# A two-layer mixture kernel on one core: its written order of issue chosen anew, with 54 engine choices changed

## The chip, the cores and the metric

The kernel runs on one core of one Trainium2 chip. The core has TensorE (PE, which multiplies matrices; its weight loads are listed as PEld), VectorE (DVE), ScalarE (ACT), GpSimd (POOL) and SyncE (SP), which here issues all loads and stores between the chip's memory (HBM) and the core's own memories: SBUF, and PSUM into which PE writes its products. The metric is the time of one execution in microseconds (us). Before the change it was 584.19 us, the median of three runs (582.6 to 584.66).

## What is computed

From `x` [4, 8, 512, 64] and `state` [4, 8, 32, 64] attention is computed in both directions; the results are joined into 4 x (512 + 32) = 2176 tokens of 512 values, and two layers follow:

```python
xread = softmax(x @ state.T / 8) @ state
sread = softmax(state @ x.T / 8) @ x
t = concat(xread, sread)               # 2176 tokens x 512
h = t @ w_in                           # 512 -> 1024
solu = h * softmax(h)
ln = (solu - mean(solu)) / sqrt(var(solu) + 1e-6) * g_ln
y = ln @ w_out                         # 1024 -> 512
h2 = y @ w2_in                         # 512 -> 2048
out = (h2 * tanh(softplus(h2))) @ w2_out   # 2048 -> 512
```

All of it is single precision. The weights arrive as 64-bit floats and are turned into 32-bit floats on the chip.

## The kernel before, in words

**Precision.** PE multiplies `fp32r` numbers, so each operand is kept as a high part and a rest (`..h` and `..l` in the names), and each product is three matmuls: low by high, high by high, high by low.

**Narrowing.** `narrow` (lines 144 to 166) makes 32-bit floats of a block of 128 x 512 words of 64 bits. The high word is rescaled (line 149 on DVE or line 151 on ACT: flag W), the low word is shifted (154 ACT, 156 DVE: flag B), and the two are joined, either by a cast on ACT (159) and one instruction on DVE (161), or by two on DVE (161, 165: flag T). The blocks of the first layer are numbered 0 to 11, those of the second 12 to 27.

**First layer.** 17 tiles of 128 tokens. Attention (lines 303 to 490) turns scores and results on DVE (STREAM_TRANSPOSE, lines 381 and 411) and leaves `aT`. `s_a0` (511) multiplies it with `w_in` (line 530). `s_a1` (535) applies softmax and normalization (lines 539 to 562; small steps on DVE, ACT or POOL by flags N and Z). `s_turn` and `s_turn_far` transpose the result: on PE, split by lines 579 and 581, or through DRAM, with a store (590) and four loads (595) for each tile. `s_d` (608) multiplies blocks of up to four tiles with `w_out` (24 matmuls, line 616) and evicts PSUM into `raw_*` by line 621, on ACT or DVE (flag X). The PSUM of `s_d`, `s_warm` and others is one ring. `s_warm` (236) multiplies unused numbers early on, so that PE is not idle: its call 0 has 26 matmuls, each further one 4, or none by flag R.

**Second layer.** The 2048 middle values are taken in eight steps `fp` of 256, and the tokens in three passes of 6, 6 and 5 tiles. In pass 0 the weights of a step are loaded (`s_load64(which, f)`, line 640: 512 KB each, `which` 0 for `w2_in`, 1 for `w2_out`, two blocks f for a step), narrowed, summed for a Strassen-Winograd scheme of 7 products (657), split into high part and rest (681, 683, 717, 719, 724, 726), and kept in DRAM for the later passes (687, 730, 733). Passes 1 and 2 fetch them from there (694, 745). Each step has 42 matmuls (`s_hp`, line 860). `s_post` (869) evicts and combines the products: `m` (line 871, ACT or DVE: flag M), `u` (874, 877), `c` (882). `s_act` (885) makes value and split (894 and 901 on ACT, 905 on DVE or POOL: flag L). Pass 0 then runs `s_po` (lines 915 to 917), with an output copy `ob` (921, flag S) and store (923). Passes 1 and 2 use sums (931, DVE or POOL: flag J), splits (939, 941), blocks (965 to 967) and running sums on DVE (972). `s_x_split` (lines 792, 794) prepares the tokens of a pass.

**What sets the order.** Nothing is scheduled by the compiler. Each engine runs its instructions in the order in which they were issued, and so does SP's queue. Every step above is a generator, which issues some instructions up to its next `yield`. All steps are listed once, and a string of two-letter codes says which is advanced next:

```python
    live = {}
    with tc.manual_schedule():
        for i in range(0, len(ORDER), 2):
            n = 64 * CODE.index(ORDER[i]) + CODE.index(ORDER[i + 1])
            if n not in live:
                step, step_args = steps[n]
                live[n] = step(*step_args)
            next(live[n], None)
```

A code that comes three times advances its step three times: `Ds` is `s_load64(0, 0)`, the load first, then the narrowing piece by piece; `DY` and `Db` are `s_d(5, 0)` and `s_d(5, 3)`, of which the last advance holds the eviction. `FLAGS` holds one character for each choice of an engine, read by `eng`:

```python
def eng(name, i, *choice):
    return choice[int(FLAGS[name][i])]
```

An instruction waits for the data that it reads and for the buffer that it writes; all later ones on the same engine or queue wait behind it.

Of the kernel before, what the change touches and what calls it, by code (L numbers as in the profile page):

```python
# [22 lines left out]
P = 128
# [60 lines left out]
    "CIDQCGCoDQCGCGCoDRB3CIDRCoB3DRB3DVCIDkDkDlDVCIDlDlDRDoDVCyDRCyDqDWDoCyDWCyDqDoDoCvCzCvDqDqCvCvDpCzDpCyDpDpCzCyCv"
    "CzCzCvC2C0C2C2C0C0DWDVC0C3DWDVC0C0DXDWDXC3C0C0C5C0C3C5C5C3C1C3C3DUDXC6C1C3C3C9C3C6C4C9C9C6C4DUDUC6C-C6C6DXC-DUC6"
    "DAC1DUC6C-C6C1C1DADAC1DXC-C4C-C-C4C4DZDrDmC4C-C-DZDBDrDaC1DaC-DBDZC_DvDwDaC4DrDrC_DaDsC1DZDaDvDYDBDvDYDvDYC4DBDw"
    "DYDBDBDZC8DvDbDwDBDBD3DbDwDsD8D8DbDYDsDbDwDsDdDmDmC_C_DdD5DxC_DxC8DdC_DxDbD9D9D3D4C7DBDeEAEAC7DxDxDdD4D6DeD5DdDt"
# [4 lines left out]
    "G3EbElG5G4EbEqEqElEfEuEuG4EfG6EbG6EcEhGwGwEcEiEfEgGvGvEcEmEcEcG1G1FLG6EkEhG0G0EjG5G4EgEpEpEkEiG2G2EjEyG4FMG5FIEm"
    "G9EtEtG4G4G9G5G9G8G-G-EfEfG8G5G5E1EoHAHAExG7EsEsG8HKExEoHKEwEwG7ExFLG_G_FLE4G7HLHFHFE4EyEyHKHLEyHGHGFLEyHKEzHMEz"
    "HDHDFIFIHLHJHJFIEzEzEzHCHCFLE3HEHEE6FAE3HMFEHBHBE6FMHMHKFJE5FIFiE7FMHKFAFAHLFME5E7HRHRHLE1FfHKHKE1FEFEFME1HSHSHL"
    "HLFNHQHQHPE1HNHcHPE2E2FVFNHcHOHdFZFZFOFNHOHHHHFNFNFJHdHIHIHPFJE2HcFJFjHOFVHcHNFOFdFdHeE2E2HNHeHWHWFJFUHTHTE_HdHU"
# [1111 lines left out]
```

## Time and profile before

| | us |
|---|---|
| median of three runs (range) | 584.19 (582.6 to 584.66) |
| the profiled execution's own time | 584.61 |
| its span in the profile | 582.8 |
| PE busy | 561.5 (96%) |
| DVE busy | 500.1 (86%) |
| ACT busy | 362.3 (62%) |
| POOL busy | 53.9 (9%) |

The profile is of one execution, whose own time is 1.8 us longer than the span that it records. Busy time of PE counts overlapping matmuls once, and their ends are modelled; whether PE is fed at its rate is read from the starts of its matmuls and from its waits. By stages, the first layer and the preparation of pass 0 fill the first 240 us or so, pass 0 of the second layer reaches to about 375 us, pass 1 to about 480 us, and pass 2 to the end.

### The profile page before, as it was taken

To read this page: it belongs to the slowest core of one execution; us is meant where nothing else is said; L and a number is where in the kernel's file an instruction comes from. 1 tells how busy PE (TensorE), PEld (TensorE's weight loads), DVE (VectorE), ACT (ScalarE), POOL (GpSimd) and SP (SyncE) were. 2 spreads that over 40 slices of the span, in tenths; PEclk is the share of its full clock that TensorE was granted. 3 is DMA by queue.
4 is the path that set the end of the run, shared out by engine and by line. 5 is a ranking of instruction groups with operands and counts; after the bars stand their busy time and mean duration, and the time that the engine had idled before them with its cause. 6 is when DMAs were issued, how large, how long until landed. Compare 5 with 4: busy or idle time off the path is not lost.

```text
span 582.8 us, 9844 instructions
## 1 busy us (share of the span) xinstructions
PE 561.5 (96%) x3561; PEld 498.6 (86%) x3561; DVE 500.1 (86%) x943; ACT 362.3 (62%) x665; POOL 53.9 (9%) x132
## 2 busy tenths in 40 slices
PE   9978999999999898999999999999999999999997
PEld 3535787899789897888888899899999998999996
DVE  5999988785787888989999997388989997989995
ACT  6997868573448765989999774443334735433340
POOL 0003222120022000000000000000000034000023
PEclk9998999999999999999999999999999999999999
DMA  8952204223215677899997889777777769987932
GB/s 349 412 204 73 73 37 128 92 74 109 73 63 191 223 283 239 305 345 336 340 325 276 323 306 321 253 280 259 250 265 254 262 246 330 338 288 289 318 113 92
DMA packets 47280, 136.05 MB, mean 233 GB/s; under 512 B 5376, under 2 KB 20864, under 8 KB 46720
## 3 DMA queue, kind: packets, MB, share of 16 engines
q1 hardware_dynamic: 47232, 135.42, 65.7%
q8 instruction: 28, 0.46, 0.3%
q14 instruction: 20, 0.16, 0.1%
HBM read 96.60 MB, written 38.80 MB: 232 GB/s over the span
## 4 chain that ended last, share of the span: by engine, by line
PE 40%; ACT 11%; DVE 2%; DMA 2%; issue 1%; ACTq 0%; DVEq 0%
PE hp L860 20%; PE po L965 6%; PE po L966 5%; PE po L967 5%; ACT w L159 3%; DMA out<-ob 2%; ACT w L151 1%; PE po L1033 1%; ACT gh L901 1%; ACT w L154 1%; ACT w2oh L724 1%; ACT w2oh L717 1%; PE po L917 1%; PE po L916 1%; PE po L915 1%
## 5 line engine op out<-in xcount | busy, mean ns | idle before, releaser
L860 PE MATMUL hp<-xo,w2r 128*128 128x384 f32 (+1 forms) x504 | 94.2, 329 | 2.2 <-DVE c L882 1.7
L860 PEld LDWEIGHTS hp<-xo,w2r 128*128 128x128 f32 x504 | 84.4, 188 | 5.8 <-DVE c L882 3.2
L860 PE MATMUL hp<-xo,w2swh 128*128 128x384 f32 (+1 forms) x336 | 83.2, 330 | 3.2 <-ACT m L871 1.5
L616 PE MATMUL pm<-ln_l,gw_hi 128*128 128x256 f32 (+1 forms) x256 | 76.3, 298 | 3.9 <-ACT raw_d L621 2.4
L616 PE MATMUL pm<-ln_h,gw_hi 128*128 128x256 f32 (+1 forms) x256 | 74.8, 292 | 0.0
L616 PE MATMUL pm<-ln_h,gw_lo 128*128 128x256 f32 (+1 forms) x256 | 74.4, 291 | 0.0
L972 DVE TENSOR_TENSOR acc<-po,acc 128x384 f32<-128x384 f32 (+1 forms) x136 | 69.0, 522 | 1.8 <-PE po L967 1.2
L860 PEld LDWEIGHTS hp<-xo,w2swh 128*128 128x128 f32 x336 | 58.9, 188 | 7.4 <-ACT m L871 2.3
L901 ACT ACTIVATE gh<-c 128x384 fp32r<-128x384 f32 (+1 forms) x57 | 29.1, 515 | 57.3 <-DVE c L882 48.1
L616 PEld LDWEIGHTS pm<-ln_l,gw_hi 128*128 128x128 f32 x256 | 48.3, 189 | 8.1 <-ACT raw_d L621 3.1
L860 PE MATMUL hp<-xo,w2swl 128*128 128x384 f32 (+1 forms) x168 | 55.1, 328 | 0.0
L882 DVE TENSOR_TENSOR c<-hp,u 128x384 f32<-128x384 f32 (+1 forms) x72 | 38.2, 532 | 13.6 <-PE hp L860 13.1
L616 PEld LDWEIGHTS pm<-ln_h,gw_hi 128*128 128x128 f32 x256 | 48.2, 188 | 0.5
L616 PEld LDWEIGHTS pm<-ln_h,gw_lo 128*128 128x128 f32 x256 | 48.6, 190 | 0.0
L939 ACT CAST qh<-t 128x384 fp32r<-128x384 f32 (+1 forms) x60 | 28.5, 489 | 31.2 <-DVE t L931 20.5
L530 PE MATMUL ph<-swh,aT 128*128 128x512 f32 x128 | 41.2, 416 | 3.7 <-ACT ph L548 2.5
L965 PE MATMUL po<-ql,w2oh 128*128 128x384 f32 (+1 forms) x120 | 39.2, 327 | 0.4 <-DVE acc L972 0.4
L966 PE MATMUL po<-qh,w2oh 128*128 128x384 f32 (+1 forms) x120 | 38.8, 323 | 0.0
L967 PE MATMUL po<-qh,w2ol 128*128 128x384 f32 (+1 forms) x120 | 38.7, 323 | 0.0
L941 DVE TENSOR_TENSOR ql<-t,qh 128x384 fp32r<-128x384 f32 (+1 forms) x60 | 31.0, 533 | 1.6 <-ACT qh L939 1.2
L860 PEld LDWEIGHTS hp<-xo,w2swl 128*128 128x128 f32 x168 | 31.5, 188 | 0.1
L530 PEld LDWEIGHTS ph<-swh,aT 128*128 128x128 f32 x128 | 23.3, 194 | 9.6 <-issue 2.7
(452 smaller groups left out, 1363.4 us busy)
## 6 DMA issues: line engine op xcount, KB each, us to landing
w2r<-ki SPq DMA_DIRECT2D x16, 768.0 KB, 6.1
w2ol<-ko SPq DMA_DIRECT2D x15, 768.0 KB, 6.5
w2oh<-ko SPq DMA_DIRECT2D x15, 768.0 KB, 6.6
w<-in_w2i SPq DMA_DIRECT2D x16, 512.0 KB, 5.7
w2swh<-ki SPq DMA_DIRECT2D x8, 896.0 KB, 6.1
w2swl<-ki SPq DMA_DIRECT2D x8, 896.0 KB, 7.0
w<-in_w2o SPq DMA_DIRECT2D x12, 512.0 KB, 5.3
ki<-w2r SPq DMA_DIRECT2D x8, 768.0 KB, 7.6
```

Source lines behind the costliest of these rows:

```text
L159: nc.scalar.copy(out=src.bitcast(F16)[..., 1], in_=f32(high))
L530: nc.tensor.matmul(out=ph[:, hf * 512:(hf + 1) * 512], lhsT=a_[:, c * P:(c + 1) * P], rhs=w_[:, q, hf * 512:(hf + 1) * 512], start=q == 0 ...
L616: nc.tensor.matmul(out=pm[:, :n], lhsT=w_[:, k, m * P:(m + 1) * P], rhs=l_[:, c0:c0 + 4 * len(blk), k, :], start=k == 0 and j == 0, stop=k ...
L860: nc.tensor.matmul(out=r, lhsT=w_[:, 0, k * P:(k + 1) * P], rhs=x_[:, k, :n], start=s in (0, 1, 3, 4) and cnt == 0, stop=cnt == 5, skip_gr ...
L882: nc.vector.tensor_tensor(out=c, in0=bank[ps, fp, s], in1=u, op=ALU.add)
L901: nc.scalar.activation(out=gh, in_=src, func=AF.Mish)
L939: nc.scalar.copy(out=hi, in_=src)
L941: on('V', ((ps - 1) * NFP + fp) * 4 + int(name[1]) - 1).tensor_tensor(out=lo, in0=src, in1=f32(hi), op=ALU.subtract)
L965: nc.tensor.matmul(out=r, lhsT=wh[:, a, c], rhs=x[1], start=first or not held, stop=False)
L966: nc.tensor.matmul(out=r, lhsT=wh[:, a, c], rhs=x[0], start=False, stop=False)
L967: nc.tensor.matmul(out=r, lhsT=wl[:, a, c], rhs=x[0], start=False, stop=last or not held)
L972: on.tensor_tensor(out=o, in0=x, in1=y, op=ALU.add)
```

## The change

Only the two constants are changed; no line of code is. In `FLAGS` 54 characters differ (B 8, J 1, L 1, M 5, N 6, Q 2, R 1, S 1, T 3, W 4, X 14, Z 8), each of which gives one operation to another engine, or, for R, leaves out one `s_warm` of 4 matmuls. `ORDER` has 3158 codes instead of 3160: the two codes of `s_warm(7)` are gone, and every other step has as many codes as before, in another sequence from the first line on. In the diff one stretch of `ORDER` is shown, with the eviction of `s_d(5, 0)` and the narrowing of `s_load64(0, 0)`; the rest is cut.

```diff
 FLAGS = dict(
...
-    B="1011001100011000000001111110",
+    B="0000011100011000010010111010",
-    J="0000000000000000000000000000010000000000000000000000000000000000",
+    J="0000000000000000000000000000000000000000000000000000000000000000",
-    L="000000000000000000000000000000000000000000000000000000000000000100000000000000000000000000000000",
-    M="000110000110100001000010",
-    N="00010010100111011",
+    L="000000000000000000000000000000000000000000000000000000000000000000000000000000000000000000000000",
+    M="001100001110000000000010",
+    N="00010001110010001",
-    Q="111111111111110001010001",
-    R="0101010101110000",
-    S="000100",
-    T="1100010110001010111111111110",
+    Q="111011111111110101010001",
+    R="0101011101110000",
+    S="000110",
+    T="1101111110001010111111111110",
-    W="0001000100000001101000000000",
-    X="10000000001000011010010000000111",
+    W="1101010100000001111000000000",
+    X="00111010001100100101010001000101",
-    Z="11111110010100001",
+    Z="11101011110011101",
...
 ORDER = (
...
-    "DYDBDBDZC8DvDbDwDBDBD3DbDwDsD8D8DbDYDsDbDwDsDdDmDmC_C_DdD5DxC_DxC8DdC_DxDbD9D9D3D4C7DBDeEAEAC7DxDxDdD4D6DeD5DdDt"
...
+    "DAC1C6C1C-C1DADAC4DUC-C4C-C-C4C4DaDrC1DmC-DZDBDrC8C-DaDmDmC-DaDrDrDaDBC_DvDwDZDaC4DZDBC_C7DsC1DYC4DBDZDBDBDYDZDv"
+    "C1DYDBDBDvDYDvDbDBDwDbDYDvDbDwD3DwDbC7D8D8D3DeDsC_DwC_DbDeC_DxD5DxDdC_DsDxD9D9DxDxDdD4EAEAC7DsDdD4D5DeDtC8DsEBEB"
...
```

Told by its instructions, the stretch has this order on ACT (the step, its line):

```
before: split_out(0,0) L717, load64(0,0) L151, d(5,0) L621, load64(0,0) L154
after:  d(5,0) L621, split_out(0,0) L717, load64(0,0) L151, d(5,3) L621
```

What moves elsewhere, in the same terms:

- ahead of `s_a0(6)`: two operations of attention, `s_front_turn(2, 0)` (lines 411 and 348), are issued later, and one split, one small step and one eviction (lines 422, 546, 621) come sooner;
- between the loads and the narrowing of the second layer's weights: most of the loads are issued sooner on SP's queue, by 1.5 to 5 us of PE's work for those of the last steps. The narrowing of some is moved further still, so that it follows more closely behind its load: for `s_load64(1, 8)`, (1, 9), (1, 7), (0, 8), (0, 6), (0, 7). For (1, 0), (0, 0), (1, 3), (0, 2) it follows at a greater distance;
- `s_load64(0, 3)` stands ahead of a store of `s_keep_out(1, 1)`, and the last reader of the slot that it fills (line 726) stands sooner on DVE;
- the stores of the outputs of pass 0's last step (line 923) stand ahead of the two loads of `s_fetch_in(1, 2)` (line 694), which come later;
- passes 1 and 2 have nearly their old order.

## Rows read from the trace of the kernel before

**Rows 1.** The page, first line and part 1: busy us (share) xinstructions.

```profile
span 582.8 us, 9844 instructions
PE 561.5 (96%) x3561; PEld 498.6 (86%) x3561; DVE 500.1 (86%) x943; ACT 362.3 (62%) x665; POOL 53.9 (9%) x132
```

**Rows 2.** Chain in order of time: start us, duration, engine, output, line, count.

```profile
400.37 2.08 PE hp L860 x12
```

**Rows 3.** By stretch: PE, PEld, DVE, ACT, POOL busy; PEclk, DMA share, GB/s.

```profile
54.00:56.00 2.00, 2.00 (x6) 1.58 (x5) 2.00 (x5) 1.81 (x4) 1.11 (x4) 0.50 0.00 0
60.00:70.00 10.00, 8.82 (x81) 7.19 (x80) 9.60 (x19) 9.14 (x15) 2.18 (x9) 1.00 0.34 107
260.00:280.00 20.00, 19.73 (x100) 17.57 (x99) 19.43 (x42) 19.84 (x34) 0.00 (x0) 1.00 0.88 332
400.00:420.00 20.00, 20.00 (x117) 20.00 (x116) 17.82 (x36) 5.70 (x13) 0.00 (x0) 1.00 0.70 254
460.00:465.00 5.00, 5.00 (x31) 4.93 (x30) 5.00 (x11) 3.30 (x7) 1.02 (x1) 1.00 0.71 280
```

**Rows 4.** Waits of PE, 90 to 380 us: us in total, times, longest.

```profile
PE pm L616 <- ACT raw_d L621: 2.4, 3, 1.7
PE hp L860 <- ACT m L871: 1.5, 1, 1.5
PE hp L860 <- DVE c L882: 1.4, 2, 0.8
PE po L965 <- ACT ob L921: 0.8, 1, 0.8
```

**Rows 5.** Waits of PE, 380 us to the end.

```profile
PE hp L860 <- ACT a__5553 L894: 0.5, 1, 0.5
```

**Rows 6.** Timeline of DVE, 61 to 75 us: start, duration [idle before].

```profile
62.26 0.70 DVE L411 STREAM_TRANSPOSE aw<-tt 128x512 f32<-128x512 f32 x1
```

**Rows 7.** Timeline of all engines, 188 to 194 us.

```profile
189.03 0.33 SPq L640 DMA_DIRECT2D w<-in_w2i  x1
...
192.34 0.68 ACT L151 ACTIVATE w<-w 128x512 f32<-128x512 f32 x1 [1.04 <-DMA w<-in_w2i]
...
192.93 0.35 ACT L621 COPY raw_d<-pm 128x256 f32<-128x256 f32 x1
...
193.33 0.39 PE L616 MATMUL pm<-ln_l,gw_hi 128*128 128x256 f32 x1 [1.71 <-ACT raw_d L621]
```

**Rows 8.** Timeline of all engines, 223.5 to 230.5 us.

```profile
224.09 0.43 DVE L149 TENSOR_SCALAR w<-w 128x512 f32<-128x512 f32 x1 [1.34 <-DMA w<-in_w2i]
...
228.38 0.61 PE L860 MATMUL hp<-xo,w2swh 128*128 128x384 f32 x2 [1.54 <-ACT m L871]
```

**Rows 9.** Timeline of ACT, 240 to 266 us.

```profile
250.82 0.53 ACT L901 ACTIVATE gh<-c 128x384 fp32r<-128x384 f32 x1 [2.45 <-DVE c L882]
...
253.71 1.37 ACT L159 CAST w<-w 128x512 f16<-128x512 f32 x1
```

**Rows 10.** DMA issues, 238 to 266 us: count, KB each, median us to landing.

```profile
w<-in_w2o SPq DMA_DIRECT2D x3, 512.0 KB, 5.8
...
room<-in_w2o SPq DMA_DIRECT2D x1, 512.0 KB, 10.3
```

**Rows 11.** Timeline of all engines, 357 to 370.6 us.

```profile
359.57 3.52 SPq L923 DMA_DIRECT2D out<-ob  x3
...
369.86 0.58 ACT L921 COPY ob<-po 128x512 f32<-128x512 f32 x1 [7.13 <-DMA out<-ob]
```

**Rows 12.** Timeline of POOL and DVE, 460 to 481 us.

```profile
463.57 1.02 POOL L905 TENSOR_TENSOR gl<-a__5227,gh 128x384 fp32r<-128x384 f32 x1 [271.41 <-DMA w2ol<-ko]
463.58 0.55 DVE L882 TENSOR_TENSOR c<-hp,u 128x384 f32<-128x384 f32 x1
...
475.17 0.49 DVE L905 TENSOR_TENSOR gl<-a__5381,gh 128x320 fp32r<-128x320 f32 x1
...
479.58 0.91 DVE L905 TENSOR_TENSOR gl<-a__5424,gh 128x320 fp32r<-128x320 f32 x1
```

More of the change, by code (lines that the diff above doesn't have):

```diff
@@ L127 @@
[L127 to L128 removed]
+    "AAAABGBGATBIBIBKBKAUAUARARAWAWBABAA0A0BHBHA-A-ATBHBHA6A6BJABABBJBPAQAQBJBOANANAYAYBLBJAJAJA2A2BLBCBCBPADADAaAaBO"
+    "BRAFAFBQBRBXA8A8BBBLBBBUBBAVAVBLBXBXA1APAPBTAXAXA1BQA1BUBBA4A4AOAOBTBSAZAZA_A_BeA7A_A7BSBUBEBEA1A7BhBhA_AbAbA3Bg"
+    "BgBDBDASASB5BDBeBeA7B5AcAcBUBUA3B5B7AeAeA9BDB6B7AgAgB5B7BVBiBiB6B7B8A3AiAiBVB6A5A9A5A9A5BbBbAdAdA3BVBYBYA9AfAfA5"
@@ new lines @@
+    "B8BfBfBFBFBaBaBVBjBZBZBFB5BjB8BVBVBVBnAhAhB6BcB7AjAjBFB6BWB6B8BdBcBWBkBkBnBWBMBqBnBdAkAkBlB8AmAmB_BNCJAoAoBdBoAq"
+    "AqBqB9BlBNCJCJB9B8B9BMBlB9BoBqBlCNCKBlB-B_BoB_CNCNBoB-B_BlCKCABlBlBrBrBlBoCKBmBmCOCKAsAsCKCKAuAuAwAwCDAyAyCOCBCR"
+    "CKBoCKCKCOCBCRCRCDBoCBBmCOBoCDBoCBCOCOBsCLCSCDB-B-CLCOCVBsCSCOBsCACVCVCSCOB_CLCACSBsCPCWCSCSAlAlBpAnAnBsApApBpCZ"
+    "CSArArCDCWBpCSB9BsBsCBCMCACWCZCZCPCSCPBsCMCQDFCWCaCWCWDFCMCaBuCWCWBvBvCQDHCQDHBuBvDHCaBvDHCCBuCaDFCaCaCTBvDFBvCT"
+    "CaDHBvBvBxDFCaCaCTCcCWBxCbCECcCcCEBxCbDGCdCfCdDGCdCACECACfCfCCCdCdCdCYCgDGCYCdCCCCCYCgCdDGAtAtBtCiAvAvCgBtAxAxCE"
@@ new lines @@
+    "AzAzCdCUBtCgCXBwCiCiCgCgCeCXDECgCjCeCUDEBwCgCXDECgDGB1CUCjBwDJCjDEB1DJCeDEChCjCeDJCjCjCeDKCbB1CeB4CjCjCbCbCjCbCm"
+    "ChB4CmCmB4CeDKCnDKCECeDKCnDJCbCnCqDJCEDKCnCqCqCbCnCnByByCrCnCnCtCnCrCFCkBzCFCtCtCFCrClBzCrDLCrCrCHDLB2CHCHDLCrCr"
+    "CuDLCHBzDMDLB2CuDICrDMBzCuDICwBzCkB2CFCsDIB2DIBzBzCsBzDMChClDIChDMB0ChCkDNChDMB0ClDOCFB0DOCuCHB2CuCuDOB2DOB2B2Cu"
+    "DNB3DNDOB3CuCwCwChB3CuChCpDNCxCIDNDPCICvCxDPDPCvCxDSDSCxCxCxDSDPCxDSCsDPCpCxCsCGCxCpCsDTDSCsDTCyDTCyDTDQDTDQCsCo"
+    "CICsCoDQCGCoDQCGCGDQDRCIDRDRDRCIDkDkDlDlDlDVCyDRDoCICyDWCyDqDoCyCzCvDqDoDoCvCvDpCvDWDqDqDVDpCzCyDpDpCyDVCzCvCvCz"
@@ new lines @@
+    "DgEJEZEZEWEEDgEEEEDgEEEFEFDgEFELEFEFELEeE0EdEbGkGkGmDnGmGnDnDnEMGmENGnENGmGoEaEaESESGnEMGoEaExGoGmEWEWEeEeGmEaEe"
+    "GnGtGtGnGrGmGmEeGqGrE0GuGuE0GqGnGnE0GsGsGrEdG4GpEdGqGpEbEdG4GpE0GyGyG5EdEnGzGzEbG5ErErG4EnE8EfEbEvEvExG4FBFBEfEx"
+    "ElEbGwGwG6EqEqE8G6GvGvExEcFFFFGxGxEcElG0G0EhFLEcEiEuEuEgEfG2G2EjEcEcG5G4EkEjEmEpEpEiG4G6EkG1G1G5FLEyHAHAG5FLEmG3"
+    "G3G8ExG9G4G4FMG9EgEfEfG8G_G_E1G5G5E4EoE4G-G-G9FLEsEsHKEhEoFIG7EtEtG8HKEyEwEwEyHLEyHFHFFLHKHLG7EyE3HKFAEzE5EzHME3"
+    "HMHGHGEzFEFMG7HEHEE5E1EzEzHKE6FMHMFME6HDHDHLFJE7HCHCHLFIFAFAHKE7FIE1FEFEFMHBHBE1FfFNHKHKFNFiFVFNHLFIHIHIFZFZHLHL"
@@ new lines @@
+    "E1HJHJHOE2HHHHHPE2HPFNFNHcFjHOFIHNE2HQHQFPHdFUE2E2HcFJFPHOE-HSHSFUE_FCFCFVHcFTFJE9FdFdHdHRHRFYFYFJE-FDFDHYHYE9FO"
+    "HXHXFGFGFWFJHeHcFWHNFfHNFaFaHWHWF5FKHeE_HTHTFfHdHVHVFfFKHPHcFHFHFOFiFeFeHeHbHbFiHdFiFKHcFKFKFfFRHiHiHdFjFRHcHcFj"
+    "I2FgFQHkHkHdHdHhFjFTHUHUFQFcFcHaHaI2HfF6I2HuFSFmFXFXFSHgHZHZFjHvF2HhHjHjFbFbFiHgHuHhFlHgFuHfHuF5HfFqHvHoHoFkF5Fv"
+    "FvFkHqHqF5FkI2HuI2FrFkFkFsHnHnFrHwFwFwFqHlHlHwHvFtGQHtHtFmFzFzFgFtHuFgHwFgF1F1HuHvI2F6HuHuHvHzI2FxFxHzHmHmFsHyHy"
+    "H2H2HvHvFlHsHsHxF6F2GRFgIAF0F0F2FhFyFhF2HrHrFhFhFhH0H0I2I2FoHyHpHpIBHzHxF5H1H1F6FoH8H8F2F3FnIAHxF9FpF6H7H7F7FuFu"
@@ new lines @@
+    "GDH4H4FnGQF9GHGHFpH5H5F8GQGDIAGNGQFyFyIBF8GLGLH6H6F7ICF7IAICF7F7GQGEH_H_ICGBGEGCIAGGGGGBGRGIGIIGIGIBF3GKGKGCIHIH"
+    "GRGMGMH3H3IBGRIFIAIFGRGSIAIAGSF3GSH-H-F3IBIIIIGSGSIBIBIEH9H9IFIEIDISIEIDF3GZININF4GNF4IMIMF4GNIDF-IOIOF4F4GNGZIJ"
+    "IJF-IPIPF_ITILILF_GAGNIRIRGOGbGFGFGAGUISGfGfGTGUGaGJGJGTGcISGYITGeGeGaGgIKIKIUGYGdGdIUISGiGiGOIUISITGbIYIYITGhGh"
+    "GOISIXGOIXGOISISGjGjITGVGPIZIZIWITITIWIXIaIaIVGPIVIkGPJAJAIWGWI-I-GPGPIQIQGWIlJdGXIgIgGVI3GcGcGXIkI3I3GgGgIkIlI7"
+    "I7IkImIVImI3I3IeIeIlI8ImIkI4I8I7IkIlI6I4IpIdIdIpIlI6IkIkIoIoI7I7I4IfIfIoJbI9I4I4JbJbIcIcI8IlIlJdJdI8I8IiIiInI9In"
@@ new lines @@
+    "IjIjIpI5IqIqI9I5I5I6IsIsI9I9I5I5IbIbInI6I6IwMmIrIrIwMmJCIwMmMmMmJCJDIxJDJCIxIxIhIhJEGlGlJEJCJBJEJBJBI_IvIvJDI_I_"
+    "IyJCIyIyJCJDJHItItJHJDJCJCJHJGJGIuIuJ6J6JDJDJ4J4JGI0JFJII1JIJJJfJIJKJIJIJLIzKXJLJfJeIzJMJeJeJgJcJYJYJMJcJcJXJXI0"
+    "I1IzJZJZI1JKJOJJJNJgJOI0JfJNJPJhJQJhJfJhJQJPJfJgJaJaJgJSJkJfJSJkJRJgJfJfJkJRJjJjJUKVJgJgJTKVKVJjJiKXKXJ8JTJlJlJm"
+    "J8JlJUJ9JoJVJmJlJlJWJVJ9J8J5JWJoJnJ5J5JpJ7JqJnJ7J7J8JpJqJ0J0J9JrJ1J1JrJ-J3J3J-J2J2J-J8J8J9KBJsKBJ9JtJsKAJ8J8KAJt"
+    "KAJuKyKyJ9J9JvK0K0JuJ_KZKCKCKDKZKCLRKaKDKFJwKCKCKFKZKGJvKGKRKRKaJxJwKZJxKBJyKaJzJyKSKSKYJzKEKHKYKYKEKWKIKHKWKWKT"
@@ L129 @@
+    "PgP7P7PJO1O4PKPJO3PhPgO4PJO6PJPJPMPgPhPNO6O3PgPNPHO5PhPPPdPLO5PbPbPdPdPPPOPKPfPaPaPfPfPOPiPRPiPLPQPRPgPQPiPgPhPM"
+    "PlPSPhPlPYPYPSPkPTPlPkPgPgPkPTPZPZPhPhPUPjPVPUP9PVPmPXPmPnPWPmP-P9PXP8P8PoPWPpP6P6PnP9PoPpPrP-PsPmPmP9PrP_PsPqPt"
+    "P_PqPuP_P9P-PtP9PtP-PuPvP-PuPwPvQBP4PwQBPxQCQBPyQCPxP3QCPzPzPyP2P0P0PzP9P9PzP1P0P-P-QDQAP0P1QAQEQDQDP1P2QFQEQAQE"
+    "P2QGP3QFQHQFPzP4QJQGQHQGP0QIQHQKQIQIQJQKQJQK"
 )
```

74 lines of the change are left out of this document (18 added, 56 removed).

## Prediction, made before the changed kernel was run

> **What bounds the kernel now.** The page's first part comes first: PE is busy for 561.5 us of a span of 582.8 [rows 1], so 21 us at most lie outside PE's work. The chain in order of time then shows what a fed PE looks like: 12 matmuls in 2.08 us, 0.174 us from start to start [rows 2]. Nearly all of pass 1 and pass 2 runs at this rate: in 400 to 420 us PE has no gap, and DVE is at 17.8 of 20 [rows 3]. So time can be had only where PE is not fed. The table by stretch shows where: in 60 to 70 us PE has 8.82 of 10 and DVE 9.60, so DVE sets the front; in 260 to 280 us PE, DVE and ACT all have 19.4 us or more of 20, with the DMA engines at 0.88 [rows 3]. PE's waits price the rest. Between 90 and 380 us the four largest groups are 2.4, 1.5, 1.4 and 0.8 us [rows 4]; after 380 us the largest is 0.5 [rows 5]. The change leaves PE's matmuls as they are, but for four, and so it can gain a few us in the front, some 6 us of waits in the middle, and almost nothing behind.
>
> **What it removes and swaps.** `s_warm(7)` goes, with four matmuls. Their duration has no row of its own; by the rate of 0.174 us for 384 columns [rows 2], four of 512 columns are 4 x 0.174 x 512/384 = 0.93 us of PE's work. In the front DVE is the fuller engine [rows 3], so I take 0 for it there (0 to -0.9). The other 53 flags trade operations in both directions: summed over the kernel with the durations of like instructions, each engine's total changes by under 2 us, DVE's and ACT's by about +1 and POOL's by -1.6. What they do is local, and stands in the terms below.
>
> **Front, to about 80 us.** DVE's queue decides when `s_a0(6)` can start. Ahead of it lie about 73 us of DVE work; two operations of attention of 0.70 us go behind it [rows 6], and a split, a small step and an eviction come in front, which leaves 0.9 us less. With a DVE that is 96% busy [rows 3] I take -0.7. The low end is -2.5, if the warm matmuls' 0.9 and a further part of PE's 1.2 us of idle time in 60 to 70 us go too; the high end is +2.0, if the two that were put off (1.4 us) hold up the attention behind them.
> A term of the front could turn on the clock. In 54 to 56 us the granted clock was 0.50, the lower of its two levels (1.2 GHz against 2.4), with PE at work on six matmuls in 2 us, while DVE had 2.00 us of 2 [rows 3]: the dip cost nothing that DVE did not take anyway. "TensorE: Matmul & The Clock Gate" in the Trainium skill, Part 1, says that the throttled state is the default one and that activity releases it, which speaks against removing warm matmuls; by it the front would lose instead of gain. That is a rival below; the sum goes by DVE.
>
> **185 to 200 us.** Here the trace shows PE waiting 1.71 us for an eviction on ACT that took 0.35 us itself; ACT stood at the rescale of `load64(0,0)`, which waited 1.04 us for a load issued 3.3 us before [rows 7]. The new order puts the eviction of `s_d(5,0)` ahead of that rescale, so this wait goes. The next one on PE's ring, `s_d(5,3)`, is now behind the same rescale, and the block of loads keeps its other work, so something of 0.4 to 1.0 us stays: -1.71 + 0.5 = -1.2. Bounds: -2.1 (all of it, and 0.4 us of slack), +0.5 (the stall moves to `s_d(5,3)` and grows).
>
> **220 to 240 us.** PE waits 1.54 us for `m`, an eviction on ACT, and DVE waited 1.34 us just before for a load of `w2_in` [rows 8]. The slot of that load, `s_load64(0,3)`, becomes free sooner and its issue passes one store on SP's queue; by DVE's order its last reader stands 0.7 to 1 us sooner. But its narrowing stands sooner as well, by 1.0 us of PE's work. I take -0.4; -1.2 if the DVE wait goes, +1.0 if the narrowing comes to it first.
>
> **240 to 340 us.** The order here takes loads as later: most of them are issued 1.5 to 5 us sooner, but their first reader follows more closely. Counted in PE's work at 0.174 us a matmul, the distance from issue to first read falls for `s_load64(1,8)` from 7.9 to 3.5 us, for (1,9) from 12.0 to 6.9, for (1,7) from 13.1 to 6.9, for (0,8) from 9.3 to 7.6. The trace has landings of 5.8 us in the middle and of 10.3 for one [rows 10]. What covers them is ACT's and DVE's other work, and ACT has idle time in places (2.45 us before the activation at 250.8 [rows 9]), though none in 260 to 280 us. Against that, two steps become lighter on ACT by about 1.6 us each (one cast of 1.37 us [rows 9] and a small one), and one grows by 3.4 us, to 15.1 us of a step of about 15.5. The known waits on `c`, 1.4 us in two places [rows 4], are the most that can go, with small ones. I take -0.5 (-2.0 to +4).
>
> **360 to 376 us.** The fourth output copy on ACT waits 7.13 us for a store, because three stores (3.52 us of SP's queue) and the fetches of 896 KB stand together [rows 11]; PE's wait of 0.8 us for `ob` follows from it [rows 4]. The stores now stand 5 to 9 us of PE's work sooner and ahead of the fetches, which come 3 us later but are read a step after. -0.8 (-1.3 to +0.3).
>
> **Passes 1 and 2.** DVE is at 5.00 us of 5 in 460 to 465 us [rows 3], and two operations move to it from POOL. On POOL they took 1.02 us each [rows 12]; on DVE the same operation of 320 columns took 0.49 us, so two of 384 columns are 2 x 0.49 x 384/320 = 1.2 us, or 0.9 if their overlap with neighbours, as seen from start to start, is taken off. PE then runs behind DVE for a few us until DVE's slack takes it up: +0.5 (0 to +1.3).
> A gain could come back here. One operation of 0.49 us on DVE took 0.91 with POOL at work [rows 12], so a POOL that has nothing would stretch nothing. "GPSIMD Engine Reference" in the Trainium skill, section 1, says that POOL shares its interface to SBUF with DVE, with contention where DVE has two inputs in SBUF; by it DVE would win back up to 2 x 0.42 us and the term would be near zero. The row of the very instruction that moves speaks against: beside the POOL operation at 463.57 DVE's `c`, which reads PSUM, took 0.55 [rows 12], not stretched. I keep +0.5, and -0.6 as the low end.
>
> **Sum.** -0.7 - 1.2 - 0.4 - 0.5 - 0.8 + 0.5 = -3.1 us against the profiled execution's own 584.61 us: 581.5 us. That execution lies 0.42 us above the median of the three runs, 584.19, so the forecast is -0.46% against the median. A measurement of this kernel tells about 0.5% from no change, 2.9 us: "faster" begins below 581.3 and "slower" above 587.1, and the forecast lies on the edge of the first.
>
> **The rivals.**
> *The stalls only move (584).* Each wait on an in-order engine that is removed may show up at the next instruction behind the same load, as `s_d(5,3)` does at 190 us. For it: PE, DVE and ACT are all full in 260 to 280 us [rows 3], so none has room for more than its share. Against it: the waits at 190 and 370 us have a nameable cause that the order takes away. With -0.7 for the front and +0.5 behind it, the time is about 584.
> *All of the waits go (577.5).* The waits of rows 4 sum to 6.1 us; with the front's -0.7 or so the time is 584.6 - 6.1 - 0.7 = 577.8, and with a part of the small ones about 577.5. For it: the loads' issues stand sooner. Against it: the rings and slots are the same.
> *Transfers lose their cover (588).* Slower than before. In 240 to 265 us ACT reaches the narrowing of (1,8), (1,9), (1,7) and (0,8) before the data is there, as it did at 192.34, and the evictions queued behind it hold PE. The price of one such case is 1.71 us [rows 7], of four 6.8: with the other terms 581.5 + 6.8 = 588.3. It decides where the distance is shorter than the landing, 3.5 to 7.6 us against 5.8 to 10.3 [rows 10]. Against it: PE's work is a lower bound for the time that passes, and (1,8)'s own load may land sooner than the mean.
> *The clock.* If the granted clock stays at 0.50 in the front past the point where DVE is the bound, matmuls take twice as long there. A 2 us stretch as in 54 to 56 us [rows 3] held one such us of work, so two stretches cost about 2 us: 583.5.
>
> **How the numbers follow.** The forecast's own case (waits at 190 and 370 us gone, little else) has 0.45; it straddles the bound of 581.3, and half of it counts as faster. All waits gone 0.18; stalls only move 0.18; the clock 0.06; cover lost 0.13. Faster: 0.23 + 0.18 = 0.41. Slower: 0.13 and 0.02 from a worse mix of the high ends, 0.15. Same: the rest, 0.44. The range from 577.0 to 587.5 takes in the best rival and most of the way to the worst, since the term of 240 to 340 us alone reaches +4.
>
> **What would show it.** Right: no wait of PE over 1 us at 185 to 200 us; no ACT wait for a store near 370 us; the front's first matmul of `s_a0(6)` sooner by about 0.7 us; the same rate of matmuls from 400 us on. Wrong: an idle time of ACT "from a DMA of w or room" in 240 to 270 us with a PE wait behind it; granted clock 0.50 after 80 us; waits of PE for DVE at 460 to 480 us of more than 1 us.

## The result, and the profile after

The changed kernel takes 576.0 us (median of four runs, 575.86 to 576.29) against 583.39 us in four runs of before: a ratio of 0.9875, 95% interval 0.9847 to 0.9903. It is faster by 1.25%, where 0.46% was forecast, and lies 1.0 us below the stated range. In the later comparisons, with 14 to 25 runs of before in each, before's median was 581.97 to 582.61 us; against these the gain is 6.0 to 6.6 us (1.0 to 1.1%). The experiments below ran on five chips; a few tenths between two runs on different chips are not read as a difference.

The page, first line and part 1, of the changed kernel:

```profile
span 574.6 us, 9808 instructions
PE 558.4 (97%) x3557; PEld 497.6 (87%) x3557; DVE 500.2 (87%) x949; ACT 364.2 (63%) x659; POOL 54.5 (9%) x134
```

DVE, ACT and POOL have no less to do, and PE only four matmuls less (against [rows 1]); the span is 8.2 us shorter. The table by stretch, with the columns of [rows 3]:

```profile
54.00:56.00 2.00, 2.00 (x10) 1.65 (x9) 2.00 (x5) 1.80 (x4) 1.25 (x6) 1.00 0.52 195
60.00:70.00 10.00, 9.59 (x96) 7.07 (x94) 9.92 (x21) 9.94 (x19) 2.70 (x10) 1.00 0.34 107
...
260.00:280.00 20.00, 20.00 (x98) 17.52 (x98) 19.52 (x41) 19.82 (x33) 0.00 (x0) 1.00 1.00 379
400.00:420.00 20.00, 20.00 (x116) 19.76 (x115) 18.08 (x37) 8.94 (x19) 0.00 (x0) 1.00 0.74 276
```

In 260 to 280 us PE now has no gap, with DVE and ACT as full as before and the DMA engines at 1.00 instead of 0.88. PE's waits between 90 and 380 us, which answer to [rows 4]:

```profile
PE hp L860 <- DVE c L882: 0.5, 2, 0.3
PE pm L616 <- ACT raw_c L621: 0.5, 1, 0.5
PE hp L860 <- ACT a__3287 L894: 0.4, 1, 0.4
PE hp L860 <- DVE u L874: 0.4, 1, 0.4
PE hp L860 <- ACT m L871: 0.4, 1, 0.4
```

The largest single wait was 1.7 us; it is 0.5 us now. To see where the span went, the starts of all matmuls were laid against PE's work: each matmul counts as the usual distance from start to start of its kind, the warm ones left out, and the two kernels are compared where the same amount of work is done. The stretches are in before's time; "clean" stands for e4 below, which is before up to 340 us, in an execution without the wait at 190 us.

| stretch (us) | forecast (range) | profile after - before | after - clean |
|---|---|---|---|
| 0 to 149 | -0.7 (-2.5 to +2.0) | -0.8 | -1.0 |
| 149 to 179 | none | +0.7 | +0.7 |
| 179 to 202 | -1.2 (-2.1 to +0.5) | -2.7 | -0.5 |
| 202 to 223 | none | -0.3 | -0.2 |
| 223 to 247 | -0.4 (-1.2 to +1.0) | -1.5 | -1.5 |
| 247 to 361 | -0.5 (-2.0 to +4) | -0.9 | -1.0 |
| 361 to 373 | -0.8 (-1.3 to +0.3) | -1.5 | (changed in e4 too) |
| 373 to 453 | none | +0.4 | |
| 453 to 505 | +0.5 (-0.6 to +1.3) | -0.8 | |
| 505 to PE's end | none | -0.4 | |
| PE's end to the span's end | none | -0.5 | |
| sum | -3.1 | -8.3 | |

Each profile is one execution, and such a number is good to a few tenths: f1 and f3 below, with the changed kernel's instructions there, have -1.0 and -2.0 where it has -1.5 (223 to 247). The +0.7 at 149 us is mostly the new wait for `raw_c` in the list above: its eviction stands behind a cast of 0.83 us on ACT.

The three places that the prediction named look like this now. At 190 us, the timeline that answers to [rows 7]:

```profile
186.80 0.33 SPq L640 DMA_DIRECT2D w<-in_w2i  x1
...
190.26 0.37 ACT L621 COPY raw_d<-pm 128x256 f32<-128x256 f32 x1
...
191.72 0.70 ACT L151 ACTIVATE w<-w 128x512 f32<-128x512 f32 x1
192.30 0.37 ACT L621 COPY raw_d<-pm 128x256 f32<-128x256 f32 x1
```

The eviction of `s_d(5,0)`, at 190.26, stands ahead of the rescale of `load64(0,0)`, at 191.72, and that of `s_d(5,3)` behind it. The rescale no longer waits: the load was issued 2.2 us sooner and landed at 189.91, 1.8 us before it. At 220 us, answering to [rows 8]:

```profile
220.37 0.43 DVE L149 TENSOR_SCALAR w<-w 128x512 f32<-128x512 f32 x1 [0.66 <-DMA w<-in_w2i]
...
223.69 0.47 ACT L871 COPY m<-hp 128x384 f32<-128x384 f32 x1
...
230.31 1.01 DVE L882 TENSOR_TENSOR c<-hp,u 128x384 f32<-128x384 f32 x2
...
232.18 0.42 DVE L149 TENSOR_SCALAR room<-room 128x512 f32<-128x512 f32 x1
```

DVE still waits for the load, but 0.66 us instead of 1.34, and two `c` stand together ahead of the narrowing of `s_load64(1,6)`. At 360 us, answering to [rows 11], the fourth copy on ACT has no wait for a store:

```profile
360.24 0.58 ACT L921 COPY ob<-po 128x512 f32<-128x512 f32 x1
...
361.98 3.65 SPq L923 DMA_DIRECT2D out<-ob  x3
```

The three stores in this line are the last three; the first three, which stood at 359.57 us before, are issued at 345 to 353 us now, ahead of the fetches, and have landed by 359.1.

### The profile page after: what moved, and what is told of

Its sections match the earlier page's. It is cut to its first block, busy times and chain, and to the rows that moved or that the text cites. A ratio compares the mean times of both kernels' runs of the same rounds, so it can differ in the third digit from the quotient of the medians.

```text
span 574.6 us, 9808 instructions
## 1 busy us (share of the span) xinstructions
PE 558.4 (97%) x3557; PEld 497.6 (87%) x3557; DVE 500.2 (87%) x949; ACT 364.2 (63%) x659; POOL 54.5 (9%) x134
## 5 line engine op out<-in xcount | busy, mean ns | idle before, releaser
L616 PE MATMUL pm<-ln_l,gw_hi 128*128 128x256 f32 (+1 forms) x256 | 77.6, 303 | 0.6 <-ACT raw_c L621 0.5
L159 ACT CAST w<-w 128x512 f16<-128x512 f32 x22 | 30.7, 1394 | 3.2 <-DVE w L156 2.8
```

What stands on the lines that cost most here:

```text
L159: nc.scalar.copy(out=src.bitcast(F16)[..., 1], in_=f32(high))
L616: nc.tensor.matmul(out=pm[:, :n], lhsT=w_[:, k, m * P:(m + 1) * P], rhs=l_[:, c0:c0 + 4 * len(blk), k, :], start=k == 0 and j == 0, stop=k ...
```

## The experiments

All ratios are to the kernel before, run beside it on the same chip: e1 to e4 on one chip, the f runs on a second, e5, s1, s2 and b1 on a third, the other g runs on a fourth, g5 and h1 on a fifth.

| run | median us | ratio (95% interval) |
|---|---|---|
| e1, choices alone | 589.7 | 1.0121 (1.009 to 1.0151) |
| e2, order alone | 584.03 | 1.0022 (1.0006 to 1.0037) |
| e3, eviction ahead | 582.25 | 0.9996 (0.9973 to 1.0018) |
| e4, fetch behind stores | 580.87 | 0.9969 (0.9951 to 0.9987) |
| e5, load sooner | 582.54 | 1.0003 (0.9983 to 1.0023) |
| s1, new until 240 us | 580.04 | 0.9955 (0.9937 to 0.9974) |
| s2, new from 240 us | 579.25 | 0.9938 (0.9915 to 0.9961) |
| f1, old first narrowing | 577.83 | 0.9925 (0.9902 to 0.9948) |
| f2, old second narrowing | 579.58 | 0.9947 (0.9928 to 0.9967) |
| f3, old POOL operations | 576.21 | 0.9895 (0.9869 to 0.9921) |
| f4, old rest of first layer | 579.21 | 0.9948 (0.9927 to 0.9969) |
| b1, m ahead | 576.72 | 0.9891 (0.9865 to 0.9917) |
| g1, tile place | 582.73 | 1.0012 (0.9993 to 1.0031) |
| g4, tile place and load | 582.44 | 0.9996 (0.998 to 1.0013) |
| g2, the moves together | 580.31 | 0.9966 (0.9954 to 0.9978) |
| g5, g2 and c ahead | 580.47 | 0.9962 (0.9947 to 0.9977) |
| g3, m and u ahead | 577.32 | 0.9911 (0.9897 to 0.9926) |
| h1, two more moves | 576.56 | 0.9902 (0.9886 to 0.9918) |

**Choices or order.** e1 is before with the new `FLAGS`, e2 the new `ORDER` with the old `FLAGS`.

> The order of before with the 54 new engine choices. Theory (the gain lies in where loads and evictions stand in the order): within 1.5 us of before, since the work of each engine changes by about 1 us in all; PE's wait of 1.71 us near 190 us, that of 1.54 us near 228 us and the output copy's wait of 7.1 us for a store near 365 us are still there. Rival (the engine choices free ACT and DVE at these places): 4 us or more below before, with two of the three waits gone. Third reading (order and choices only fit each other): slower than before by 1 us or more.

> The new order with the old engine choices (the call of the warm matmuls that the new order leaves out is left out here too). Theory (the gain lies in the order): 5 us or more below before, with the three waits of 1.71, 1.54 and 0.8 us of PE gone or under 0.6 us. Rival (the engine choices): less than 3 us below before. Third reading (they only fit each other): no gain, new waits of PE on evictions of 1 us or more.

Both theories fell; the third reading holds. The choices alone cost 7.2 us (589.7 - 582.5), the order alone 1.5, and both together gain 6 or more. The front shows a part of it; PE's largest waits for the narrowed weights of the first layer, from 0 to 95 us, in e1:

```profile
PE ph L493 <- DVE w_in_t L161: 3.7, 3, 2.7
```

and in e2:

```profile
PE ph L493 <- DVE w_in_t L165: 1.8, 1, 1.8
PE ph L493 <- DVE w_in_t L161: 1.8, 1, 1.8
```

A piece of the first layer's weights comes too late in both: the order was written for the engine that narrows it. By 95 us e1 is 5.3 us behind before. e2 is only 0.2 behind before there, 1.7 behind the changed kernel; it loses 2.8 us more between 95 and 179 us and 1.0 between 247 and 361.

**Which choices.** In the changed kernel one set of characters at a time was put back:

```diff
 f1:  T at 3, 4, 6;  B at 0, 2, 3, 5;  W at 0, 1, 5
 f2:  B at 17, 20, 21, 25;  W at 17;  M at 2, 4, 8, 12, 17
 f3:  L="...1..." and J="...1..." (the two operations on POOL again)
 f4:  X, N, Z, Q as before
```

> The changed kernel with the old engine choices for the narrowing of the first layer's weights alone (T at 3, 4, 6, B at 0, 2, 3, 5, W at 0, 1, 5). Theory (order and choices were made for each other, each stage by its own choices): the front loses 1.3 to 2.5 us by 100 us, with waits of PE for w_in_t of about 2 us each near 22 and 30 us as with the new order alone, and nothing is lost behind. Rival (the loss of the new order alone in the front came of the small steps and evictions, X, N, Z and Q): within 0.5 us of the changed kernel.

> The changed kernel with the old engine choices for the narrowing of the second layer's weights (B at 17, 20, 21, 25, W at 17) and for the eviction m (M, five places). Theory (as above): 2.5 to 4 us lost between 220 and 300 us, with PE waits near 223 and 236 us on m and near 273 us on gl, as with the new order alone; nothing lost before 220 us. Rival (the new order gains there by where it puts the loads, whatever engine narrows): under 1 us lost.

> The changed kernel with the two operations of pass 1 (L905 of s_act(1,7,1,1), L931 of s_tsum(1,7)) back on POOL. My reckoning before the result: DVE is full there, so 0.5 us is gained by giving them away. Rival A (POOL stretches DVE's operations beside it): 0.3 to 0.8 us lost, with DVE's neighbours of 0.55 us at 0.9 us. Rival B (PE has slack over DVE there): within 0.2 us; the 0.7 us that 450 to 500 us gained are then of the order.

> The changed kernel with the old engine choices for the rest of the first layer: the evictions (X, 14 places), the last and a small step of the normalization (N, Z) and the scalings of attention (Q). Theory: 0.5 to 2 us lost between 60 and 200 us, with new waits of PE on evictions (L621) or on the transposed result (L581, L579). Rival (these choices have slack enough either way): within 0.4 us.

Against the profile of the changed kernel f1 loses 1.5 us by 45 us, nothing more before 220, and 0.5 by 240; f2 nothing clear up to 245 us and 2.2 by 300; f4 0.8 near 98 us, 0.5 near 165, 1.0 between 190 and 250, and 0.8 behind PE's end. By medians these are 1.8, 3.6 and 3.2 us above 576.0, and 1.6, 3.4 and 3.0 above f3, which ran on the same chip and no run of which is as slow as the fastest of f1, f2 or f4. So each set is worth 1.6 us or more, mostly at its own stage, in this order. The three sums make 8.0 us, as much as the order alone lies above the changed kernel (584.03 - 576.0): the sets act each by itself. In f2 the largest wait between 220 and 300 us is a new one, of `gl` on DVE:

```profile
PE po L917 <- DVE gl L905: 1.1, 1, 1.1
```

f3 is equal to the changed kernel to within 0.2 us: rival B. DVE's neighbours beside these two operations of POOL are not stretched; the addition at 457.60, which reads PSUM, took 0.56 us:

```profile
457.15 1.02 POOL L905 TENSOR_TENSOR gl<-a__5233,gh 128x384 fp32r<-128x384 f32 x1 [268.57 <-DMA w2ol<-ko]
...
457.60 0.56 DVE L882 TENSOR_TENSOR c<-hp,u 128x384 f32<-128x384 f32 x1 [0.28 <-PE hp L860]
```

Elsewhere in f3 a DVE operation with both inputs in SBUF is: beside POOL's sums it took 1.30 us, where the like take 0.48.

```profile
478.29 1.01 POOL L972 TENSOR_TENSOR ob<-acc 128x384 f32<-128x384 f32 x1
478.35 1.30 DVE L941 TENSOR_TENSOR ql<-t,qh 128x320 fp32r<-128x320 f32 x1
```

**Two halves.** s1 and s2 join the two orders at the first matmul of `s_hp(0,1)`: one string up to there, then the other without what was done already, each part with its own choices.

> The new order and choices up to the first matmul of s_hp(0,1) (about 235 us), and from there the remaining steps in the order of before, with its choices. Against an execution of before without the wait of 1.71 us at 190 us the changed kernel is 2.4 us ahead at this point. Theory (stages are independent, the gain of each is its own): 2 to 3 us below before's median, with the waits of before behind 240 us (about 0.8 us each near 288, 307 and 362 us). Rival (the later stages' gain hangs on how far the loads are ahead when they begin): 1 us or less below, or 4 us or more below.

> The converse: the order and choices of before up to the first matmul of s_hp(0,1), and from there the new ones. Theory (independent stages): 3 to 4 us below before's median, which with the converse makes the 6 to 6.5 us between the medians; the wait of 1.5 to 2.0 us near 224 us is there, those behind 240 us are not. Rival (what the later stages gain hangs on the first): under 2 us below.

s1 is 2.6 us below before's 582.6, s2 3.4, together 5.9 of the 6 to 6.6 us. Within the noise the two stages are independent; the unit that has to fit is the stage with its choices.

**The wait at 190 us.**

```diff
-D3 Db Dw Ds D8 D8 Db DY Ds
+D3 DY Db Dw Ds D8 D8 Db Ds
```

> The kernel before with one move: the eviction of s_d(5,0) on ACT ahead of the rescale of load64(0,0). My reckoning before the result: PE's wait of 1.71 us goes, 0.4 to 1.0 us comes back at s_d(5,3), whose eviction still stands behind the same rescale: 0.7 to 1.3 us gained by the stretch 185 to 205 us. Rival A (the order of the eviction is all that counts): 1.7 us or more gained. Rival B (the late landing of load64(0,0), which comes of the store before it in the queue, is what counts; the eviction's place only names who suffers): 0.5 us or less gained, with a wait of 1.2 us or more at the next eviction.

The timeline of ACT in e3 shows the eviction ahead and a rescale that hardly waits:

```profile
189.10 0.38 ACT L621 COPY raw_d<-pm 128x256 f32<-128x256 f32 x1
189.70 0.69 ACT L151 ACTIVATE w<-w 128x512 f32<-128x512 f32 x1 [0.21 <-DMA w<-in_w2i]
```

But e4, which has the old order here, has nearly the same:

```profile
190.33 0.69 ACT L151 ACTIVATE w<-w 128x512 f32<-128x512 f32 x1 [0.44 <-DMA w<-in_w2i]
190.92 0.35 ACT L621 COPY raw_d<-pm 128x256 f32<-128x256 f32 x1
```

In the profiled execution of before `s_load64(1,0)` was issued at 179.67 us and landed after 6.79 us; in e3, e4, e5, s2, g1, g2 and g5, with the same instructions and an issue within 0.2 us of that, it landed after 4.15 to 4.82, and in g4 after 5.56. Behind it a store of `s_turn_far(15)` took 6.25 us instead of 3.7 to 4.2 (5.0 in g4), and `s_load64(0,0)` waits for this store, whose slot it fills. By 202 us the profile of before is 2.0 to 2.3 us behind e4, e5, s2 and g1, and 1.4 behind g4. So the wait of 1.71 us was mostly of that one execution and came of the late landing, as rival B has it; its wait at the next eviction did not show.

By medians the move itself is worth nothing (0.9996). At 202 us the profile of e3 is 0.9 us ahead of that of e4, partly because `s_load64(1,0)` landed 0.8 us sooner; by 247 us 0.2 of it is left. The timeline of DVE in e3 shows where it went: `c` stands behind the narrowing of `s_load64(1,6)`, which was issued 1.3 us sooner than in e4 and landed no sooner (232.86 and 233.02 us).

```profile
232.88 0.43 DVE L149 TENSOR_SCALAR room<-room 128x512 f32<-128x512 f32 x1 [1.42 <-DMA room<-in_w2o]
233.23 0.55 DVE L882 TENSOR_TENSOR c<-hp,u 128x384 f32<-128x384 f32 x1
```

**The outputs at 360 us.**

```diff
-J4 J4 JD JD J6 J6 Ix ... Iy
+JD JD Ix ... Iy J4 J4 J6 J6
```

> The kernel before with one move: the two fetches of 896 KB of s_fetch_in(1,2) on the queue behind the third of the output stores of pass 0's last step instead of ahead of the first. Theory (the stores land late because they share the transfers with these fetches): the stores land 3 to 5 us after their issue instead of 7.7 to 9.5, the fourth output copy waits under 3 us, PE's waits of 0.98 and 0.27 us near 370 us go, about 1.2 us gained. Rival (the stores are late because the copies themselves stand late in the order): no more than 0.4 us gained. Slower if the fetched weights come after PE wants them at about 379 us: a wait of PE there of more than 1 us.

The theory holds. In the timeline of e4 the stores go first and land 2.1 to 3.2 us after their issue, the fourth copy waits 0.74 us for PE and for no store, and 1.5 us are gained on PE between 361 and 373 us:

```profile
357.57 3.52 SPq L923 DMA_DIRECT2D out<-ob  x3
...
361.18 0.38 SPq L694 DMA_DIRECT2D w2swh<-ki  x1
361.48 0.59 ACT L921 COPY ob<-po 128x512 f32<-128x512 f32 x1 [0.74 <-PE hp L860]
```

This one move gains 0.31% by itself, and 1.5 us is all that the changed kernel gains in this stretch.

**The wait for m at 224 us.** Five kernels take the stretch apart, all on the order of before:

```diff
 e5
-EP EQ EI EI EY EY Dh EP ER EE ER
+EP EI EI EP EE EQ EY EY Dh ER ER
 g1: the two codes of s_keep_out(0,0,2), D-, behind those of s_keep_out(0,1,2), EC
 g4: e5 and g1;  g2: e3, e4 and g4
 g5, in g2
-Gm Gm E0 Gr Gn Gr ... E0 Gu Gu Gn Gn
+Gm Gm Gn Gn E0 Gr Gr ... E0 Gu Gu Gn
```

> The kernel before with one move: on DVE the last reader (L726 of s_split_osum(1,0)) of the slot that s_load64(0,3) fills ahead of L719 of s_split_out(1,1), and the load's issue ahead of the two stores of s_keep_out(1,1,1). Theory (PE's wait of 1.5 to 2.0 us for m near 224 us is the end of a chain that begins with this load's landing): the load is issued 0.6 to 1.0 us sooner, lands as much sooner, and the stretch 220 to 240 us gains 0.6 to 1.0 us. Rival (the chain on ACT ahead of m, a split and a cast of 0.83 us, sets the wait): under 0.3 us gained.

The load landed at 220.78 us, and the split and the cast followed; but ACT stood idle for 1.78 us between the cast and `m`. The timeline of ACT in e5:

```profile
223.40 0.83 ACT L792 CAST xo<-raw_a 128x768 fp32r<-128x768 f32 x1
226.01 0.48 ACT L871 COPY m<-hp 128x384 f32<-128x384 f32 x1 [1.78 <-issue]
```

"issue" means that the profile shows nothing that ended it. In the transfers' records the store `s_keep_out(1,1,2)` lands 0.07 us before `m` starts, in before, e3, e4, e5 and s2 alike. In that order the compiled program puts `m`'s tile over the one that this store reads.

> The kernel before with one move: the store s_keep_out(0,0,2) behind s_keep_out(0,1,2), so that the tile of the sums of s_split_osum(1,1) falls into another of the four buffers, and m's tile no longer lies over it. Theory (in the order of before m waits for the store s_keep_out(1,1,2), which reads that tile and lands 0.07 us before m starts, in every profile of that order): m follows the cast ahead of it with less than 0.1 us between, and no longer 0.07 us behind that landing; since the landing of s_load64(0,3) still holds the split and the cast ahead of m, only the idle time of 0.3 to 0.6 us goes. Rival (ACT's idle time ahead of m is a fetch of its code): the idle time stays at the same instruction.

> The move of the tile together with the earlier load of e5_load_sooner, which alone gained nothing. Theory (two things end last together, the store under m's tile and the load behind the split): 1.0 to 1.8 us gained in 220 to 240 us, PE's wait for m 0.8 us or less instead of 1.8 to 2.1. Rival (a third thing holds m): a wait of 1.5 us or more stays and under 0.4 us is gained.

> The kernel before with the moves of e3, e4, e5 and the tile together: the fetch behind the stores, the eviction ahead, the load sooner and m's tile elsewhere. Theory (places are independent): 2.5 to 3.5 us below before's median, about half of the whole change. Rival (they are not): under 1.6 us, which the fetch behind the stores gains alone.

The tile is the cause of the idle time: with it elsewhere, `m` follows the cast at once in g1, g4 and g2, and the store lands 0.35 to 1.5 us after `m` has begun. In the changed kernel too the tile lies elsewhere, and `m` starts 2.4 us before that store lands. PE's wait for `m` falls from 1.5 us before to 0.7 in g4 and 0.2 in g2. And still neither gains time over its parts; g2, between its theory and its rival at 2.25 us below before, is within the noise no better than e4 alone (0.9966 and 0.9969). The timeline of g2 shows where it went:

```profile
232.96 0.43 DVE L149 TENSOR_SCALAR room<-room 128x512 f32<-128x512 f32 x1 [1.51 <-DMA room<-in_w2o]
233.30 0.55 DVE L882 TENSOR_TENSOR c<-hp,u 128x384 f32<-128x384 f32 x1
...
235.78 0.45 PE L860 MATMUL hp<-xo,w2r 128*128 128x384 f32 x1 [1.51 <-DVE c L882]
```

As in e3, `c` stands behind a narrowing that waits for `s_load64(1,6)`: issued 1.8 us sooner than in e4, it landed at 232.94 us, no sooner than there.

> g2_three_places with one more move: the second and third c of s_post(0,0) on DVE ahead of the narrowing of s_load64(1,6), which waits for its load (in g2 DVE stood idle for 1.5 us before it, with these c behind). Theory (what the load and tile moves gained at m was lost again at c, because c stands behind a narrowing whose load lands at its own time; in the new order c stands ahead of it): PE's wait of 1.68 us for c near 234 us falls to 0.4 us or less, and the time to 1.0 to 1.6 us below g2. Rival (the wait passes on to the next thing, the split of the loaded block): within 0.4 us of g2.

With `c` ahead the wait is gone; the timeline of DVE in g5:

```profile
231.43 0.55 DVE L882 TENSOR_TENSOR c<-hp,u 128x384 f32<-128x384 f32 x1
232.32 0.56 DVE L882 TENSOR_TENSOR c<-hp,u 128x384 f32<-128x384 f32 x1 [0.33 <-PE hp L860]
232.90 0.43 DVE L149 TENSOR_SCALAR room<-room 128x512 f32<-128x512 f32 x1
```

At the first matmul of `s_hp(0,1)` 1.6 us are gained over g2, 0.5 us of them are left by 260 us, and the median is the same (580.47 and 580.31). The rival holds: the delay passes on, now to `gl`. Four moves by hand did not bring together the 1.5 us that the whole new order gains here.

**Further than the change.** Three kernels move single instructions in the changed one:

```diff
 b1 -Gm Dn Gm Gn Dn Dn              +Gm Gm Gn Dn Dn Dn
 g3 -Gm Dn Gm Gn Dn Dn EM Gm EN Gn  +Gm Gm Gn Gn Dn Dn Dn EM Gm EN
 h1 -Ee Ee Gm Ea Ee Gn Gt Gt Gn     +Ee Ee Gm Gn Ea Ee Gt Gt Gn
    -Fk Fk Fs Hn Hn Fr Hw           +Fk Fk Hw Fs Hn Hn Fr
```

> The changed kernel with one more move: the eviction m of s_post(0,0) on ACT ahead of the cast of 0.83 us of s_x_split(0,2). If the wait of 0.5 us for m near 223 us and the one for u behind it come of that cast: 0.4 to 0.8 us gained. If the operand that the cast begins is wanted as soon: nothing gained, a wait for xo of 0.5 us or more takes its place.

> The changed kernel with m on ACT and u on DVE ahead of the cast and the subtraction of s_x_split(0,2); with m alone ahead the wait moved on to u (1.14 us). If it ends there: 0.4 to 1.0 us below the changed kernel. If the next one behind u takes it up: within 0.3 us.

> The changed kernel with two moves at its largest remaining waits behind 220 us: the first c of s_post(0,0) ahead of a join of s_load64(0,4) on DVE (PE waits 0.50 us there), and s_act(0,4,0,0) ahead of a split of 0.67 us on ACT (PE waits 0.57 us). If nothing takes their place: 0.6 to 1.0 us below the changed kernel. If each only passes its delay on: within 0.3 us.

None is faster than 576.0. In b1 the wait for `m` went and those for `u` and `c` grew; in g3 it moved on to `a`; in h1 a wait for another `c` came in place of the first one (0.4 us), and the one for `a` near 289 us stayed at 0.4. No version was found that is faster than the changed kernel.

## Why the prediction was wrong

**The frame was right, the sizes were not.** PE is fed at the same rate where it was, and what was gained are its waits; the direction was right at every place that the sum names but 453 to 505 us. The rival "all of the waits go (577.5)" came nearest and had 0.18. That is partly luck: its 6.1 us of waits, and the 584.61 us from which both it and the forecast start, hold some 2 us that only the profiled execution had; later medians of before are 582.0 to 582.6.

**The step that failed first** is "The other 53 flags trade operations in both directions ... What they do is local, and stands in the terms below". The terms below held few of them: three small operations of the front (lines 422, 546 and 621), ACT's balance in 240 to 340 us and the two of POOL. The three do not come sooner in DVE's order, as the text ahead of the prediction has it; their choices give them to DVE. f1, f2 and f4 show 1.6 to 3.6 us for each of three sets, and e1 and e2 that neither half of the change works alone. Equal totals on each engine were read as a price of zero, where the place of one late narrowing decides.

**The front** came out in its number (-0.9 at 80 us, -0.8 at 149, against -0.7) and in its sign: the first matmul of `s_a0(6)` starts at 80.71 us instead of 81.44. But the reason, less DVE work ahead of it, is not what decides. The instructions issued ahead of it on DVE fill 71.8 us in before and 70.9 in the changed kernel; in f1 they fill 70.9 as well, in e2 70.7, and there it starts at 82.16 and 82.40, later than before. The choices for narrowing the first layer's weights, which had no term, make the difference. The hit is luck.

**220 to 240 us** was the worst-sized of the terms with the right sign: -0.4 with a bound of -1.2, measured -1.5. The prediction priced the one wait of 1.54 us [rows 8] through its load. The place holds a chain, for `m`, `u`, `a` and `c`, and behind `m` lie a store that the profile does not name and a second load, `s_load64(1,6)`. e5, g1, g4, g2 and g5 show these links, and that one link alone gives nothing. How the rest of the 1.5 us is made up stays open.

**185 to 200 us**: -2.7 in the profiles, but the step is wrong in kind. A wait of one execution was taken for a standing one. Some 2.0 us of the 8.3 between the two profiles come of it; the other 6.3 agree with the medians.

**360 to 376 us**: right mechanism, confirmed by e4; the term was -0.8 and measured -1.5, since all the small gaps around the named wait went too.

**453 to 505 us**: +0.5 forecast, -0.8 measured, the term that had its sign wrong. In the order of before the two operations seem to cost what was reckoned: e1, with the new choices in that order, loses 0.8 us between 462 and 474 us. In the new order f3 shows them to be worth 0.2 us at most. The gain is made near 488 us, where two waits of PE go. The changed kernel, e2, f3 and s2 have neither, e1 and e4 have both; in before (PE's waits, 440 to 520 us):

```profile
PE hp L860 <- ACT a__5553 L894: 0.5, 1, 0.5
PE hp L860 <- DVE c L882: 0.4, 1, 0.4
```

So it is the order's. The prediction had the first of them in [rows 5] and gave it no term. DVE at 5.00 of 5 [rows 3] was read as a bound, but PE had slack over it in the new order. The sentence on "GPSIMD Engine Reference" in the Trainium skill was rightly left out of the sum: no stretching by POOL shows beside these two operations. Where both inputs of DVE lie in SBUF the trace agrees with it: 1.30 us instead of 0.48 at 478.35 in f3.

**Cover lost (588)** did not come, but it was near. In the changed kernel `s_load64(1,8)`, (1,9), (1,7) and (0,8) were first read 0.08, 2.7, 0.8 and 1.3 us after they landed (5.5, 6.5, 3.6 and 1.8 in before), 3.9 to 8.3 us after their issue. ACT waited 0.7 us for the first of them, with no wait of PE behind it. The reads were put just behind the landings. The landings of these four were shorter than the prediction's 5.8 to 10.3 us [rows 10]: 3.8 to 7.0.

**The clock** cost nothing. With one warm call fewer the granted clock was 1.00 in 54 to 56 us. It is not the change's doing: f4, with the same calls, had 0.50 there and stood level with the changed kernel at 97 us, and g4, in the order of before, had 1.00. What "TensorE: Matmul & The Clock Gate" in the Trainium skill, Part 1, says of a throttled default is not contradicted; removing this warm call did not bring it about.

## What to carry to other kernels

In a hand-written order, the choice of engine and the place in the queue are one decision: price them together, and do not take equal totals as no effect. Before a single wait is priced, look at the same place in a second execution, and at what stands behind it: in a stage where three engines are full, a wait that goes is worth what the next one leaves. An idle time that nothing ends may be a tile that a store is still reading.

## What the runs showed of the hardware

The same 512 KB load, issued at the same time behind the same instructions, landed after 4.15 to 4.82 us in seven executions, after 5.56 in one and after 6.79 in one, and the last moved the span by 2 us. Another, `s_load64(1,6)`, was issued 1.3 and 1.8 us sooner in e3 and g2 than in e4 and landed at the same time. The last three stores of the kernel landed 1.8 us after their issue in the changed kernel and 2.4 to 2.6 us after in before, and so the span ended 3.4 or 3.9 us behind PE. That is not shown to be the change's: s1, with before's order there, had 1.8, and f4, with the new one, 2.7 for the last. A DVE operation with two inputs in SBUF took up to 1.30 us beside POOL instead of 0.48, one that reads PSUM 0.56 as ever. The dip of the granted clock near 55 us (0.50 instead of 1.00) comes and goes between executions, in both orders.
